# Reordering the seven-product passages of a fused linear-attention and feed-forward kernel

## The chip, the cores and the metric

The kernel runs on one core of a Trainium2 chip. The metric is the device time of one execution in microseconds (us); before the change it is 678.05 us, the median of three runs (677.73 to 678.31). The core has five engines with their own instruction queues: TensorE (PE in the profile, its weight loads PEld), VectorE (DVE), ScalarE (ACT), GpSimd (POOL, here only an issuer of DMAs) and SyncE (SP, also an issuer of DMAs). TensorE writes to PSUM[...].

## What is computed

The reference is a linear attention with decay, whose output is the input of a feed-forward block:

```python
for b in range(nb):                       # blocks of 64 positions, per batch and head
    intra = (qb @ kb.T * Dmask) @ vb
    inter = (qb * lam_pow) @ kv_state
    out[block b] = intra + inter
    kv_state = lam_block * kv_state + (kb * rev_pow).T @ vb
x = out.transpose(0, 2, 1, 3).reshape(3072, 512)
h = x @ w_in                              # 3072 x 2048
g = h - tanh(h)
y = g @ w_out                             # 3072 x 512
```

There are 4 batches, 8 heads, 768 positions and heads of 64; all data are fp32.

## The kernel before

**Groups.** The 3072 tokens are worked on in 6 groups g of 128 positions in 4 batches, 512 tokens each. The attention of group g+1 is cut into pieces (`p0`, `p1`: transposes, scores, outputs, state, sums) that are run between the feed-forward products of group g.

**Seven products.** From group 1 on, each of the two feed-forward products is made by a scheme of Strassen's kind: both factors are cut into 2 x 2 quarters, and seven products of sums of quarters, called P1 to P7 here, take the place of eight. `FACT` (L386) names the factors: P1 = A11 B11, P2 = A12 B21, P3 = S4 B22, P4 = A22 T4, P5 = S1 T1, P6 = S2 T2, P7 = S3 T3. The first product (`up`, L406) is made in four units u of 512 hidden columns. The second (`down`, L602) takes each of its seven products over all units at once.

**Inner seven products.** Some of the seven are cut once more. In the first product from group 2 on, P2 and P4 are made so, for all four units together, ahead of the units (`inner`, L487): seven steps in the order 1, 2, 6, 5, 7, 3, 4 (`STEPS`), step by step for P2 and P4 in turn, P2 with PSUM bank `yb`, P4 with bank `ya`. Their results go to the hidden blocks 11 and 21, which unit 0's P1 and P7 then add to. In the second product P3 to P7 are made so (`down_twice`, L649), with few exceptions (`twice`, L522: P3 and P7 in group 1, P3 in group 5 are plain). Steps 1, 6, 7 and 4 write one y bank in turn (`ya` or `yb`), and ScalarE copies each out (L664); steps 2, 5 and 3 use bank `z` or `w`. Before step 3, VectorE subtracts in place (L666).

**Sums.** `sums_twice` (L641) makes on VectorE what an inner product needs: s1 (L644), s2 (L645), and a21 in place (L646). `sums_once` (L597) makes S2 in place of A11 from S1 (in `down` of P2, L634), and S4 in place of A12 (L801). A last operation of `up` (L454) makes S1 of a unit.

**Weights of the second product.** They come from DRAM in pieces of 256 KB, through a ring of 7 buffers `wb` (`piece`, L565), in the order of one list, `stream`, that `pieces_of` (L525) writes out. GpSimd issues the load of piece i+7 when piece i has been read. A step of an inner product eats one piece, a quarter of a plain product one.

**Order.** The loop from L770 sets the program order of a group: the units; the sums for P4; P2; attention outputs; P4; attention transposes; P5; scores; P6; outputs and state; P7; tokens for the inner products (`inner_tokens`, L475); P3; the next group's `inner`; its unit 0's P1. The scheduler may put an instruction ahead of another on its engine when the latter has to wait, unless the program demands their order; the order found is fixed when the kernel is built. Tiles with few buffers set further waits: each of the banks `ya`, `yb`, `z`, `w` is one, tag `att` has four, the output tiles `o` four, the sums four. P2 of the second product is read out of bank `w` by L632.

**Factors made on the chip.** In groups 1 and 2, `factors_twice` makes the weights of the inner products from their quarters and writes them to DRAM, at set steps of the units (`turns`, L766).

Of the kernel before, what the change touches and what calls it, by code (L numbers as in the profile page):

```python
# [13 lines left out]
AF = mybir.ActivationFunctionType  # L14
AL = mybir.AluOpType
# [8 lines left out]
def kernel(  # L24
# [459 lines left out]

    STEPS = (1, 2, 6, 5, 7, 3, 4)

    def inner(g):  # L487

        y, w, z, r5 = {}, {}, {}, {}
        for n, tag in zip(INNER, ("yb", "ya")):  # L490
            y[n] = bank("y3", tag, 1)
            w[n], z[n] = (bank(x, "att", 4) for x in ("w3", "z3"))
            r5[n] = otile("r5")
        for x in STEPS:
            for n in INNER:
                out4 = hidden(g, 11 if n == 2 else 21)
                c11, c12, c21, c22 = (out4[:, :, i, ts(j, 128)] for i in range(2) for j in range(2))
                b = toks[g, n][x]
                wb = piece(g, ("in", n), x) if x in (3, 5, 6) else None
                dst = w[n] if x == 2 else z[n] if x in (3, 5) else y[n]  # L500
                for u in range(NU):
                    a = wb.rearrange("p m c -> p (m c)")[:, ts(u, 128)] if wb is not None else a_quarter(
                        n, u, *{1: (0, 0), 2: (0, 1), 7: (1, 0), 4: (1, 1)}[x])
                    nc.tensor.matmul(out=dst[:, ts(u, 128)], lhsT=a, rhs=b, start=x in (1, 2, 5) and u == 0, stop=True,  # L504
                                     skip_group_check=True)
                d = dst.rearrange("q (u c) -> q u c", u=NU)
                if x in (1, 4, 6):
                    nc.scalar.activation({1: c11, 4: c21, 6: c12}[x], d, AF.Copy)  # L508
                elif x == 5:
                    nc.scalar.activation(r5[n], dst, AF.Copy)  # L510
                elif x == 7:
                    nc.vector.tensor_tensor(c22, r5[n].rearrange("q (u c) -> q u c", u=NU), d, op=AL.add)
                else:
                    c = c11 if x == 2 else c12
                    nc.vector.tensor_tensor(c, c, d, op=AL.add)

# [3 lines left out]
    def twice(g, n):  # L522
        return n in TWICE and not (g == NG - 1 and n == 3) and not (g == 1 and n in (7, 3))

    def pieces_of(g):  # L525
        if g >= GI:
            yield from ((g, ("in", n), x) for x in (6, 5, 3) for n in INNER)
        if g == 2:
            yield from ((g, ("quarter", t), x) for t in (3, 4) for x in range(4))
        for n in (1, 2, 4, 5, 6, 7, 3):  # L530
            yield from ((g, n, x) for x in (SUB if twice(g, n) else range(NU)))

    stream = [x for g in range(1, NG) for x in pieces_of(g)]
    sent = {"n": 0}
# [67 lines left out]
    def down(g, n):  # L602

        if n in (1, 2):
            t, first = product_bank(("down", g), n)
        else:
            t, first = bank("plain", "w" if n == 7 else "z", 1).rearrange("q (m c) -> q m c", m=2), True
        a = hidden(g, HIDAT[FACT[n][0]])
        for u in range(NU):
            wb = piece(g, n, u)  # L610
            for m in range(2):
                for kt in range(2):
                    nc.tensor.matmul(out=t[:, m, :], lhsT=a[:, u, kt, ts(m, 128)], rhs=wb[:, kt, :],  # L613
                                     start=first and u == 0 and m == 0 and kt == 0, stop=u == NU - 1 and kt == 1,
                                     skip_group_check=True)
        t = t.rearrange("q m c -> q (m c)")
        if n == 1:
            res[g, 1] = otile("q1")
            nc.scalar.activation(res[g, 1], t, AF.Copy)
        elif n == 7:  # L620
            o = otile("q7")
            nc.vector.tensor_tensor(res[g, 4], res[g, 4], t, op=AL.add)
            store(g, 21, res[g, 4])
            nc.vector.tensor_tensor(o, res[g, 5], t, op=AL.add)
            store(g, 22, o)
        elif n == 3:
            o = otile("q3")
            nc.vector.tensor_tensor(o, res[g, 5], t, op=AL.add)
            store(g, 12, o)
        else:  # L630
            o11 = late["pool"].tile([128, 512], F32, name="o11", tag="o11", bufs=1)
            nc.vector.tensor_tensor(o11, res[g, 1], t, op=AL.add)  # L632
            store(g, 11, o11)
            sums_once(g, 11, "S1", 11)  # L634

    def quarter(g, n):

# [11 lines left out]
    def down_twice(g, n, zw):  # L649
        a11, a12, a21, a22 = quarter(g, n)  # L650
        s1, s2 = low.pop((g, n))
        y = bank("y2", "ya" if n in (4, 6, 3) else "yb", 1)[:, 0:128]
        zw = bank("zw", zw, 1)
        o = res[g, n] = otile(f"q{n}")
        r5 = late["pool"].tile([128, 128], F32, name="r5", tag="r5", bufs=2)
        for x, a, dst, keep in ((1, a11, y, o[:, 0:128]), (2, a12, zw[:, 0:128], None), (6, s2, y, o[:, 128:256]),
                                (5, s1, zw[:, 128:256], r5), (7, a21, y, o[:, 384:512]), (3, a12, zw[:, 128:256], None),
                                (4, a22, y, o[:, 256:384])):
            wb = piece(g, n, x).rearrange("p m c -> p (m c)")
            for u in range(NU):  # L660
                nc.tensor.matmul(out=dst, lhsT=a[:, u, :], rhs=wb[:, ts(u, 128)], start=x in (1, 2) and u == 0,  # L661
                                 stop=u == NU - 1, skip_group_check=True)
            if keep is not None:
                nc.scalar.activation(keep, dst, AF.Copy)  # L664
            if x == 2:
                nc.vector.tensor_tensor(a12, a12, s2, op=AL.subtract)  # L666
        nc.vector.tensor_tensor(o[:, 384:512], o[:, 384:512], r5, op=AL.add)
        nc.vector.tensor_tensor(o[:, 0:256], o[:, 0:256], zw[:, 0:256], op=AL.add)
        if n == 6:

            nc.vector.tensor_tensor(o, o, res[g, 1], op=AL.add)
            for x in (4, 5):
                nc.vector.tensor_tensor(res[g, x], res[g, x], o, op=AL.add)
        elif n == 7:
            nc.vector.tensor_tensor(res[g, 4], res[g, 4], o, op=AL.add)
            store(g, 21, res[g, 4])
            nc.vector.tensor_tensor(o, o, res[g, 5], op=AL.add)
            store(g, 22, o)
        elif n == 3:
            nc.vector.tensor_tensor(o, o, res[g, 5], op=AL.add)  # L680
            store(g, 12, o)

    def down_end(g):

# [78 lines left out]
    late["pool"] = ctx.enter_context(tc.tile_pool(name="late", bufs=1))  # L763


    turns, made = {1: (0, (7, 14, 21)), 2: (7 * NU, (2, 7))}, []  # L766
    load_quarters(0)
    load_quarters(1)
    up(1, 0, 1)
    for g in range(1, NG):  # L770
        last = g == NG - 1
        p0, p1 = attention(g + 1) if not last else ([], [])
        for u in range(NU):
            for n in (2, 6, 5, 7, 1, 4, 3) if g < GI else (6, 5, 1, 7, 3) if u + 1 < NU else (6, 5, 7, 1, 3):
                if n != 1:
                    up(g, u, n)
                elif u + 1 < NU:
                    up(g, u + 1, 1)
                else:
                    down(g, 1)  # L780
                if g in turns:
                    made.append(n)
                    step = len(made) - turns[g][0]
                    if step in turns[g][1]:
                        t = turns[g][1].index(step) + len(turns[1][1]) * (g - 1)
                        if t > 2:
                            load_quarters(t)
                        factors_twice(t)
                        if t == 0:
                            load_quarters(2)  # L790
# [2 lines left out]
            if not last and u > 1:  # L793
                run(p0[u - 2:u - 1])
        sums_twice(g, 4)
        down(g, 2)
        run(p0[2:])
        sums_twice(g, 5)
        down_twice(g, 4, "z")
        run(p1[0:1])  # L800
        sums_once(g, 21, 21, 11)  # L801
        sums_twice(g, 6)
        down_twice(g, 5, "w")
        run(p1[1:2])
        if twice(g, 7):
            sums_twice(g, 7)
        down_twice(g, 6, "z")
        if twice(g, 3):
            sums_twice(g, 3)
        run(p1[2:])  # L810
        if twice(g, 7):
            down_twice(g, 7, "w")
        else:
            down(g, 7)
        if not last:
            if g + 1 >= GI:
                inner_tokens(g + 1)
            else:
                up(g + 1, 0, 1)
            if twice(g, 3):  # L820
                down_twice(g, 3, "z")
            else:
                down(g, 3)
            if g + 1 >= GI:
                inner(g + 1)
                up(g + 1, 0, 1)
        else:
            down_end(g)


# [28 lines left out]
```

## Time and profile before

| | |
|---|---|
| Time, median of 3 | 678.05 us |
| Profiled span | 678.3 us |
| TensorE busy | 662.7 us |
| Weight loads busy | 575.2 us |
| VectorE busy | 482.0 us |
| ScalarE busy | 201.3 us |
| DMA, mean over the span | 191 GB/s |
| `wb<-fine`, 154 loads of 256 KB, issue to landing | 4.1 us |

The page is one profiled execution. Busy time is time in which the engine had an instruction of the program in hand; matmuls overlap, so the distance from start to start tells more than their durations. "A<-B" is what an instruction writes and reads. In a timeline the columns are start, time, engine, line, operation, tiles, shape and count; in brackets stands how long the engine was idle before, and what ended the wait. A matmul of the program appears as two records. A step of an inner product is thus 8 records of 128 columns.

### The profile page before, as it was taken

The numbers are of one execution on the slowest core, as the hardware profiler recorded it, in microseconds if no ns is written. First come the engines' busy times: TensorE is split into PE (matmuls) and PEld (weight loads), VectorE is DVE, ScalarE is ACT, GpSimd is POOL, SyncE is SP. The second block draws the span as 40 slices with busy tenths as digits, with TensorE's granted clock in tenths as the row PEclk, the third lists the DMA queues.
The fourth block names the chain that finished last, engine by engine and source line by source line (L and its number), as shares of the span: only waits on it lengthen the run. The fifth ranks groups of instructions, "written<-read, shape, count | busy, mean of one in ns | idle before, by whom it ended". The sixth has DMA issues, their size and how long they took to land.

```text
span 678.3 us, 12940 instructions
## 1 busy us (share of the span) xinstructions
PE 662.7 (98%) x4832; PEld 575.2 (85%) x4832; DVE 482.0 (71%) x878; ACT 201.3 (30%) x398; POOL 201.5 (30%) x348
## 2 busy tenths in 40 slices
PE   6899999999999999999999999999999999999997
PEld 5788855558888899988999988899988899988897
DVE  3797858894889962588986378887358977357753
ACT  2664432423331211343112343112333122334120
POOL 0001424216444434421345200255300244500261
PEclk9999999999999999999999999999999999999999
DMA  9869979958957978686698641698821676700494
GB/s 187 227 195 236 287 215 257 301 142 248 263 173 215 259 208 202 160 238 136 180 277 266 192 82 43 153 284 244 246 42 36 153 240 206 249 22 1 112 303 159
DMA packets 162957, 129.59 MB, mean 191 GB/s; under 512 B 133904, under 2 KB 135056, under 8 KB 162896
## 3 DMA queue, kind: packets, MB, share of 16 engines
q0 software_dynamic: 29216, 97.28, 45.6%
q1 hardware_dynamic: 133536, 31.50, 23.4%
q8 instruction: 38, 0.62, 0.4%
q14 instruction: 23, 0.19, 0.1%
q10 hardware_dynamic: 144, 0.00, 0.0%
HBM read 104.34 MB, written 24.38 MB: 190 GB/s over the span
## 4 chain that ended last, share of the span: by engine, by line
PE 69%; issue 15%; POOL 6%; DMA 6%; DVE 3%; ACT 1%; SPq 0%; POOLq 0%; DVEq 0%; ACTq 0%
PE y L415 13%; PE op L719 8%; PE z L415 8%; PE y L661 7%; PE h L703 6%; PE zw L661 5%; POOL wb L578 5%; PE y L504 3%; PE w L613 3%; PE y L613 3%; PE sp L313 3%; DMA wb<-fine 2%; PE plain L613 2%; DMA raw<-in_moe_w_in_dram 2%; PE op L364 2%
## 5 line engine op out<-in xcount | busy, mean ns | idle before, releaser
L578 POOL DMA_DIRECT2D wb<-fine x154 | 82.9, 538 | 122.0 <-PE y L661 46.3
L423 ACT ACTIVATE th<-g 128x512 f32<-128x512 f32 x76 | 47.3, 630 | 104.5 <-DVE g L428 35.6
L581 POOL DMA_DIRECT2D wb<-factors x52 | 28.2, 543 | 162.0 <-PE y L613 118.1
L415 PE MATMUL y<-xt,w 128*128 128x256 f32 x320 | 73.5, 380 | 0.0
L415 PEld LDWEIGHTS y<-xt,w 128*128 128x128 f32 x320 | 60.5, 190 | 9.4 <-ACT g L508 0.9
L424 DVE TENSOR_TENSOR g<-g,th 128x512 f32<-128x512 f32 x76 | 52.0, 689 | 22.5 <-ACT th L423 22.2
L664 ACT ACTIVATE q<-y 128x128 f32<-128x128 f32 x88 | 24.4, 277 | 115.8 <-PE y L661 114.0
L703 PE MATMUL h<-xt,w 128*128 128x256 f32 x256 | 56.2, 381 | 1.1 <-DVE w L270 1.1
L719 PE MATMUL op<-wt,g 128*128 128x512 f32 x128 | 56.5, 596 | 0.0
L703 PEld LDWEIGHTS h<-xt,w 128*128 128x128 f32 x256 | 48.3, 190 | 8.5 <-DVE w L270 1.5
L661 PE MATMUL y<-wb,g 128*128 128x128 f32 x408 | 54.4, 278 | 1.0 <-DMA wb<-fine 1.0
L661 PEld LDWEIGHTS y<-wb,g 128*128 128x128 f32 x408 | 49.3, 192 | 2.4 <-issue 1.5
L719 PEld LDWEIGHTS op<-wt,g 128*128 128x128 f32 x128 | 23.8, 190 | 27.7 <-issue 26.5
L415 PE MATMUL z<-tt,ws 128*128 128x256 f32 x160 | 38.7, 380 | 0.0
L317 DVE TENSOR_TENSOR ss<-sp,mask 128x512 f32<-128x512 f32 x48 | 30.8, 681 | 10.6 <-PE sp L313 10.6
L415 PE MATMUL y<-tt,ws 128*128 128x256 f32 x160 | 38.2, 382 | 0.0
L415 PE MATMUL z<-xt,ws 128*128 128x256 f32 x160 | 37.9, 380 | 0.0
L661 PE MATMUL zw<-wb,g 128*128 128x128 f32 x272 | 36.1, 276 | 0.6 <-DMA wb<-fine 0.5
L197 POOL DMA_DIRECT2D raw<-in_moe_w_out_dram x16 | 8.8, 553 | 92.7 <-ACT r L261 59.9
L613 PE MATMUL w<-wb,g 128*128 128x256 f32 x160 | 35.8, 382 | 0.0
L613 PE MATMUL y<-wb,g 128*128 128x256 f32 x160 | 35.4, 379 | 0.0
L415 PEld LDWEIGHTS y<-tt,ws 128*128 128x128 f32 x160 | 30.1, 190 | 5.4 <-DVE g L428 1.5
(169 smaller groups left out, 1290.5 us busy)
## 6 DMA issues: line engine op xcount, KB each, us to landing
wb<-fine POOLq DMA_DIRECT2D x154, 256.0 KB, 4.1
wb<-factors POOLq DMA_DIRECT2D x60, 256.0 KB, 4.4
raw<-in_moe_w_out_dram POOLq DMA_DIRECT2D x16, 512.0 KB, 5.1
v_nat<-in_v_dram SPq DMA_DIRECT2D x24, 256.0 KB, 5.3
factors<-wt POOLq DMA_DIRECT2D x8, 768.0 KB, 5.5
wb<-fine_in POOLq DMA_DIRECT2D x24, 256.0 KB, 5.4
k_nat<-in_k_dram SPq DMA_DIRECT2D x20, 256.0 KB, 5.4
raw<-in_moe_w_in_dram SPq DMA_DIRECT2D x8, 512.0 KB, 5.8
```

Source lines behind the costliest of these rows:

```text
L313: nc.tensor.matmul(out=sp[j][:, p, :], lhsT=kt[ts(j, 64), p, :], rhs=qt[ts(j, 64), p, :], start=True, stop=True)
L317: nc.vector.tensor_tensor(ss[:, j], sp[j], mask[:, j], op=AL.mult)
L415: nc.tensor.matmul(out=t[:, m, :], lhsT=wt[:, kt, ts(m, 128)], rhs=x[:, kt, :], start=first and m == 0 and kt == 0, stop=kt == 1, skip_gro ...
L423: nc.scalar.activation(th, src, AF.Tanh)
L424: nc.vector.tensor_tensor(dst(c), src, th, op=AL.subtract)
L578: nc.gpsimd.dma_start(out=t.rearrange("p m c -> p (m c)"), in_=fine[TWICE.index(n_), SUB.index(x_)].rearrange("p u c -> p (u c)"))
L581: nc.gpsimd.dma_start(out=t, in_=factors[XAT[FACT[n_][1]]][:, 2 * x_:2 * x_ + 2, :])
L613: nc.tensor.matmul(out=t[:, m, :], lhsT=a[:, u, kt, ts(m, 128)], rhs=wb[:, kt, :], start=first and u == 0 and m == 0 and kt == 0, stop=u = ...
L661: nc.tensor.matmul(out=dst, lhsT=a[:, u, :], rhs=wb[:, ts(u, 128)], start=x in (1, 2) and u == 0, stop=u == NU - 1, skip_group_check=True)
L664: nc.scalar.activation(keep, dst, AF.Copy)
L703: nc.tensor.matmul(out=hm[:, m, :], lhsT=w1[u][:, i, a, ts(m, 128)], rhs=xt[0, t][:, i, :], start=m == 0 and i == 0, stop=i == KI - 1, ski ...
L719: nc.tensor.matmul(out=obank[b], lhsT=g, rhs=wt[:, 2 * a:2 * a + 2, :], start=kt == 0 and a == 0, stop=kt == KH - 1 and a == 1)
```

## The change

It puts four things in another order and leaves every matmul as it is.

- P2 of the second product is made between P4 and P5, no longer ahead of P4. The sums for S2 (`sums_once(g, 11, "S1", 11)`) leave `down` and are called behind P4. The list of weight pieces follows.
- The inner P2 and P4 of the next group's first product are no longer made in turn with each other. `inner` becomes a generator for one of them, `inner_steps`. P2 is made step by step in turn with P3 of the second product, which also becomes a generator.
- P4 follows, in turn with P1, P6 and P5 of unit 0, which leave the first round of the unit loop. Both inner products use bank `yb`.
- The steps at which group 2 makes its factors move by one (`turns`).

It is meant to spread the demand for weight pieces over more of TensorE's time, and to put other work between operations that share a bank.

```diff
-    def inner(g):
-        y, w, z, r5 = {}, {}, {}, {}
-        for n, tag in zip(INNER, ("yb", "ya")):
...
+    def inner_steps(g, n, tag):
+        y, w, z, r5 = bank("y3", tag, 1), bank("w3", "att", 4), bank("z3", "att", 4), otile("r5")
...
+            yield
...
+    def in_turn(g):
+        if twice(g, 3):
+            return [a for x in STEPS for a in (("down", x), ("in", x))]
+        return [("down", 0), ("in", 1), ("in", 2), ("down", 1), ("in", 6), ("in", 5), ("down", 2), ("in", 7), ("in", 3),
+                ("down", 3), ("in", 4)]
...
     def pieces_of(g):
         if g >= GI:
-            yield from ((g, ("in", n), x) for x in (6, 5, 3) for n in INNER)
+            yield from ((g, ("in", 4), x) for x in (6, 5, 3))
...
-        for n in (1, 2, 4, 5, 6, 7, 3):
+        for n in (1, 4, 2, 5, 6, 7):
             yield from ((g, n, x) for x in (SUB if twice(g, n) else range(NU)))
...
-    turns, made = {1: (0, (7, 14, 21)), 2: (7 * NU, (2, 7))}, []
+    turns, made = {1: (0, (7, 14, 21)), 2: (7 * NU, (1, 6))}, []
...
-            for n in (2, 6, 5, 7, 1, 4, 3) if g < GI else (6, 5, 1, 7, 3) if u + 1 < NU else (6, 5, 7, 1, 3):
+            for n in (2, 6, 5, 7, 1, 4, 3) if g < GI else (1, 7, 3) if u == 0 else (6, 5, 1, 7, 3) if u + 1 < NU else (
+                    6, 5, 7, 1, 3):
...
         sums_twice(g, 4)
-        down(g, 2)
+        every(down_twice(g, 4, "z"))
         run(p0[2:])
+        sums_once(g, 11, "S1", 11)
         sums_twice(g, 5)
-        down_twice(g, 4, "z")
+        every(down(g, 2))
         run(p1[0:1])
...
+        p3 = down_twice(g, 3, "z") if twice(g, 3) else down(g, 3)
+        p2 = inner_steps(g + 1, 2, "yb")
+        for kind, _ in in_turn(g):
+            next(p3 if kind == "down" else p2)
+        every(p2)
+        every(p3)
+        p4 = inner_steps(g + 1, 4, "yb")
+        for n in (None, None, 1, None, None, 6, None, None, 5, None):
+            if n is None:
+                next(p4)
             else:
-                up(g + 1, 0, 1)
...
+                up(g + 1, 0, n)
+        every(p4)
```

More of the change, by code (lines that the diff above doesn't have):

```diff
@@ L485 @@
     STEPS = (1, 2, 6, 5, 7, 3, 4)
-    def inner(g):
-        y, w, z, r5 = {}, {}, {}, {}
-        for n, tag in zip(INNER, ("yb", "ya")):
-            y[n] = bank("y3", tag, 1)
-            w[n], z[n] = (bank(x, "att", 4) for x in ("w3", "z3"))
-            r5[n] = otile("r5")
-        for x in STEPS:
[L495 to L515, printed above, removed]
@@ new lines, in inner_steps @@
+    def inner_steps(g, n, tag):
+        y, w, z, r5 = bank("y3", tag, 1), bank("w3", "att", 4), bank("z3", "att", 4), otile("r5")
+        out4 = hidden(g, 11 if n == 2 else 21)
+        c11, c12, c21, c22 = (out4[:, :, i, ts(j, 128)] for i in range(2) for j in range(2))
+        for x in STEPS:
+            b = toks[g, n][x]
+            wb = piece(g, ("in", n), x) if x in (3, 5, 6) else None
+            dst = w if x == 2 else z if x in (3, 5) else y
+            for u in range(NU):
+                a = wb.rearrange("p m c -> p (m c)")[:, ts(u, 128)] if wb is not None else a_quarter(
+                    n, u, *{1: (0, 0), 2: (0, 1), 7: (1, 0), 4: (1, 1)}[x])
+                nc.tensor.matmul(out=dst[:, ts(u, 128)], lhsT=a, rhs=b, start=x in (1, 2, 5) and u == 0, stop=True,
+                                 skip_group_check=True)
+            d = dst.rearrange("q (u c) -> q u c", u=NU)
+            if x in (1, 4, 6):
+                nc.scalar.activation({1: c11, 4: c21, 6: c12}[x], d, AF.Copy)
+            elif x == 5:
+                nc.scalar.activation(r5, dst, AF.Copy)
+            elif x == 7:
+                nc.vector.tensor_tensor(c22, r5.rearrange("q (u c) -> q u c", u=NU), d, op=AL.add)
+            else:
+                c = c11 if x == 2 else c12
+                nc.vector.tensor_tensor(c, c, d, op=AL.add)
+            yield
@@ L523, in twice @@
         return n in TWICE and not (g == NG - 1 and n == 3) and not (g == 1 and n in (7, 3))
+    def in_turn(g):
[3 more added lines that the diff above has]
+                ("down", 3), ("in", 4)]
     def pieces_of(g):
         if g >= GI:
-            yield from ((g, ("in", n), x) for x in (6, 5, 3) for n in INNER)
+            yield from ((g, ("in", 4), x) for x in (6, 5, 3))
         if g == 2:
             yield from ((g, ("quarter", t), x) for t in (3, 4) for x in range(4))
-        for n in (1, 2, 4, 5, 6, 7, 3):
+        for n in (1, 4, 2, 5, 6, 7):
             yield from ((g, n, x) for x in (SUB if twice(g, n) else range(NU)))
+        if g == NG - 1:
+            yield from ((g, 3, x) for x in range(NU))
+            return
+        for kind, x in in_turn(g):
+            if kind == "down":
+                yield g, 3, x
+            elif x in (3, 5, 6):
+                yield g + 1, ("in", 2), x
     stream = [x for g in range(1, NG) for x in pieces_of(g)]
@@ L615, in down @@
                                      skip_group_check=True)
+            if u + 1 < NU:
+                yield
         t = t.rearrange("q m c -> q (m c)")
@@ L633, in down @@
             store(g, 11, o11)
-            sums_once(g, 11, "S1", 11)
+        yield
     def quarter(g, n):
@@ L666, in down_twice @@
                 nc.vector.tensor_tensor(a12, a12, s2, op=AL.subtract)
+            if x != STEPS[-1]:
+                yield
         nc.vector.tensor_tensor(o[:, 384:512], o[:, 384:512], r5, op=AL.add)
@@ L681, in down_twice, with every @@
             store(g, 12, o)
+        yield
+    def every(steps):
+        for _ in steps:
+            pass
     def down_end(g):
@@ L779 @@
                 else:
-                    down(g, 1)
+                    every(down(g, 1))
                 if g in turns:
@@ L802 @@
         sums_twice(g, 6)
-        down_twice(g, 5, "w")
+        every(down_twice(g, 5, "w"))
         run(p1[1:2])
@@ L806 @@
             sums_twice(g, 7)
-        down_twice(g, 6, "z")
+        every(down_twice(g, 6, "z"))
         if twice(g, 3):
@@ L810 @@
         run(p1[2:])
[L811 to L817, printed above, removed]
-            else:
-                up(g + 1, 0, 1)
[L820 to L828, printed above, removed]
+        every(down_twice(g, 7, "w") if twice(g, 7) else down(g, 7))
+        if last:
+            down_end(g)
+            continue
+        inner_tokens(g + 1)
+        p3 = down_twice(g, 3, "z") if twice(g, 3) else down(g, 3)
[8 more added lines that the diff above has]
+                next(p4)
+            else:
+                up(g + 1, 0, n)
+        every(p4)
 _INS = ['q', 'k', 'v', 'lam', 'moe_w_in', 'moe_w_out']
```

## The prediction

> **What bounds the kernel now.** I read the page first, its busy line and its chain.
>
> ```profile
> PE 662.7 (98%) x4832; PEld 575.2 (85%) x4832; DVE 482.0 (71%) x878; ACT 201.3 (30%) x398; POOL 201.5 (30%) x348
> ...
> PE 69%; issue 15%; POOL 6%; DMA 6%; DVE 3%; ACT 1%; SPq 0%; POOLq 0%; DVEq 0%; ACTq 0%
> ```
>
> TensorE is the bound, and the diff leaves its matmuls as they are: every product keeps its count and shape. So the change can only remove or add holes in TensorE's stream. I looked for the holes in the PE timeline from 155 us on (group 1 to the end). A matmul record of 128 columns starts 0.112 us after the one before, one of 256 columns 0.216 us (medians of start to start), so a step of an inner product (8 records) takes 0.89 us and a 512-row product 6.9 us; what exceeds that is a hole, together with the some 0.1 us that the next record is late. The page's own waits name only the largest:
>
> ```profile
> PE zw L661 <- issue: 1.4, 1, 1.4
> ...
> PE y L661 <- DMA wb<-fine: 1.0, 1, 1.0
> PE zw L661 <- DMA wb<-fine: 0.5, 1, 0.5
> ```
>
> Summed with the smaller ones, in us: group 1, in P4 and P5 of the second product, 0.33 (228.0), 0.41 (232.8), 1.62 (235.1), and 0.35 at the state product (249.9); group 2, 0.30 (299), 0.49 over P5 (340 to 343), 0.37 in P3 (367); group 3, 0.17 in P5 (446) and 1.22 in P3 (475.5); group 4, 0.23; group 5, 0.76 in P7 (665); and 0.24 in each of four passages to the next group, where unit 0's P6 waits for VectorE to read P1's bank. That is 7.2 us: 670.8 is the floor of any gain.
>
> Two of them, as the timelines have them. Group 3's P3, last step, late because its weight piece had not landed:
>
> ```profile
> 474.76 1.06 PE L661 MATMUL zw<-wb,g 128*128 128x128 f32 x8
> 476.80 1.13 PE L661 MATMUL y<-wb,g 128*128 128x128 f32 x8 [0.98 <-DMA wb<-fine]
> ```
>
> And the largest, which is not a weight at all. P5's step 3 in group 1 reads what L666 makes, and L666 stands on VectorE behind a transpose that waits for a block of k:
>
> ```profile
> 234.75 0.71 DVE L293 STREAM_TRANSPOSE kt<-k_blk 128x512 f32<-128x512 f32 x1 [1.41 <-DMA k_nat<-in_k_dram]
> 235.39 0.65 DVE L303 TENSOR_TENSOR qd<-qt,fwd 128x512 f32<-128x512 f32 x1
> 235.96 0.68 DVE L666 TENSOR_TENSOR gS<-gS,s 128x512 f32<-128x512 f32 x1
> ```
>
> TensorE starts that step at 236.74, just after.
>
> [...] the start-to-start times above leave only 7.2 us of holes, so I go by those. [...] L666 above sat behind a stalled transpose. [...] the rows here have 676 to 693, and back to back they follow every 0.60 us. [...] The second inner product of the passage is made on one y bank instead of two, with other work between its steps.
>
> **The change part by part.**
>
> *P3 in turn with the next group's P2.* Removed: P3's seven steps alone, each eating one 256 KB piece in 0.89 us, with six more pieces behind them. Now P3's 7 pieces and P2's 3 are spread over 14 steps of 0.89 us. The pieces land a median 4.1 us after issue, up to 5.9 in group 3, and the ring of 7 gives 7 x 0.89 = 6.2 us of notice where every step eats a piece; with 10 pieces in 14 steps it gives 8.7 us. Group 3's 1.22 and group 2's 0.37 go: **-1.6**. Each y bank has three other steps (2.7 us) between its uses, as before for P2, and its evacuation takes 0.60 us on ScalarE: free. P2 writes hidden block 11, whose last reader, P6, is long past: free. Its VectorE adds fall where VectorE has little (6.4 us busy in 371 to 391): free. Its spare tile r5 waits for the store of quarter 21 to land (366.70 to 371.50 in group 2); its copy comes 7.1 us after P7's end, at about 372, so a wait of up to 0.5 us on ScalarE, with P3's copies behind it, whose bank is needed only 3 steps on: nothing.
>
> *P4 in turn with unit 0.* Between P1 and P6 now stand two steps of P4 (1.8 us), in which VectorE reads P1's bank (L428, 0.69): four times 0.24, **-0.95**. P4's first step shares bank yb with P2's last, whose copy takes 0.60 us; in the trace unit 0's P5 already slips in ahead of P1 in the same situation (277.86), so I cost it at nothing; the other end is 0.7 four times.
>
> *P2 of the second product between P4 and P5.* Its four slow pieces (1.73 us each) now let the ring fill ahead of P5, P6, P7: P5's holes in groups 2 and 3 go, **-0.65**. In group 5 the hole of P7 (0.76) comes at the end of 21 fast steps instead of 28: I take it, **-0.75**, other end 0.
>
> What it adds is that P4 starts right behind the scores, where VectorE makes P4's sums. Group 2 before:
>
> ```profile
> 318.25 0.69 DVE L645 TENSOR_TENSOR s<-s,g 128x512 f32<-128x512 f32 x1
> ...
> 320.13 0.69 DVE L451 TENSOR_TENSOR g<-g,z 128x512 f32<-128x512 f32 x1 [0.60 <-PE z L415]
> 321.58 0.69 DVE L424 TENSOR_TENSOR g<-g,th 128x512 f32<-128x512 f32 x1 [0.76 <-ACT th L423]
> 322.19 0.68 DVE L317 TENSOR_TENSOR ss<-sp,mask 128x512 f32<-128x512 f32 x1
> 322.79 0.68 DVE L454 TENSOR_TENSOR gS<-g,g 128x512 f32<-128x512 f32 x1
> ...
> 324.59 1.28 DVE L317 TENSOR_TENSOR ss<-sp,mask 128x512 f32<-128x512 f32 x2
> 325.79 0.68 DVE L646 TENSOR_TENSOR g<-g 128x512 f32<-128x512 f32 x1
> ```
>
> P4 would start at 322.0, where P2 did. Step 6 (323.8) finds s2 made at 318.9. Step 7 (due 325.6) needs L646, which overwrites what L454 must read first and comes after four score products: done at 326.5, so 0.9 us late in groups 2, 3 and 4. The attention products (L358, 1.03 us) are ready then and can stand in for it; I take a third of 2.7: **+0.9**, ends 0 and 2.7. P5's step 2 now waits for L632 to read bank w, P2's: 0.89 us of step 1 against 0.69 plus whatever stands before it on VectorE: **+0.2** in all, ends 0 and 0.6 each in four groups.
>
> Group 1 is worse off:
>
> ```profile
> 212.15 0.69 DVE L424 TENSOR_TENSOR g<-g,th 128x512 f32<-128x512 f32 x1 [0.76 <-ACT th L423]
> ...
> 217.97 0.68 DVE L644 TENSOR_TENSOR s<-g 128x512 f32<-128x512 f32 x1
> 218.57 0.68 DVE L600 TENSOR_TENSOR g<-gS,g 128x512 f32<-128x512 f32 x1
> 219.17 0.68 DVE L645 TENSOR_TENSOR s<-s,g 128x512 f32<-128x512 f32 x1
> ```
>
> There P4 would start at 212.6 and want s2 at 214.4, and s2 is done at 219.9: 5.5 us, of which the attention products (L358 and L364, 3 us) can fill the larger part. But P5's step 3 was bound by the block of k at 234.75 anyhow, so a delay of some 2 us before it runs into the 2.4 us of holes that stood there. I take **0**; ends -1.6 (the sums are made earlier) and +3.6 (L632 gets behind that transpose: P5's step 2 at about 236.7 instead of 231.1, with the four steps that had filled the wait, 3.6 us, still to come).
>
> Sum: -1.6 - 0.95 - 0.65 - 0.75 + 0.9 + 0.2 = -2.85: 678.05 - 2.85 = **675.2**.
>
> **The rivals.** *Fuller gain:* group 1's holes close as well (-1.6), and none of the +1.1 comes: 678.05 - 3.95 - 1.6 = 672.5. For it: the order on TensorE bends around waits already. Against: k lands when SyncE's queue brings it. *Even:* the ring's holes go, but P4's sums cost their full 2.7 and group 5's hole stays: -2.85 + 1.8 + 0.75 = -0.3, 677.75. For it: the 0.9 us is read straight from rows. *VectorE becomes the bound behind P4 (the other side):* group 1 +3.6, L646 +2.7, L632 4 x 0.6 = 2.4, against -3.95: +4.75, 682.8. For it: VectorE has no gap from 321.6 to 333.6[...], and in group 1 the k transposes can be placed ahead of L632, since they are ready to go while P2 still runs. Against: after that stretch VectorE has 12 us of work in the 18 us to P2's new end, so it should be free for L632.
>
> **How the numbers follow.** Forecast 0.46, fuller gain 0.10, even 0.14, slower 0.30. The slower case reaches from +1.5 (group 1 alone, partly) to +8, so half of it lies under 681.8; the range goes from 671.8, just under the fuller gain, to 681.8. Faster 0.56, same (within 1.36 us) 0.14, slower 0.30.
>
> **What would show it.** Right: no wait of P3 for a weight piece in groups 2 and 3; the passage without the wait for L428; P5 without holes in groups 2 and 3. Wrong: a hole at P4's step 6 in group 1 longer than 2.5 us, holes at P4's step 7 near 0.9 in groups 2 to 4, P5's step 2 waiting for L632, L632 behind L293 in group 1. If TensorE's busy time without holes changes by over 1 us, switching between shapes costs something that I set at nothing.

## The result: slower, and where the profile after puts the time

The changed kernel takes **687.27 us** (median of four runs, 686.68 to 688.76), the kernel before 677.89 in four runs beside it (677.07 to 678.31): a ratio of 1.0143 [1.0123, 1.0163]. The forecast was 675.2, the range ended at 681.8; it is the side of the third rival, by more than that rival gave.

The page of the kernel after, its busy line and its chain:

```profile
PE 667.6 (97%) x4832; PEld 578.7 (85%) x4832; DVE 481.1 (70%) x878; ACT 200.9 (29%) x398; POOL 201.5 (29%) x348
...
PE 85%; issue 8%; DMA 3%; POOL 2%; DVE 1%; ACT 1%; SPq 0%; POOLq 0%; ACTq 0%
```

TensorE has the same 4832 records, but they keep it busy 4.9 us longer than before: a part of the loss isn't idle time at all. The rest shows in TensorE's waits (columns: microseconds in all, number of waits, longest):

```profile
PE y L674 <- ACT r L677: 2.1, 3, 0.7
PE zw L674 <- DVE s L657: 1.9, 1, 1.9
PE w L624 <- DMA wb<-factors: 0.8, 1, 0.8
PE y L415 <- ACT g L443: 0.7, 1, 0.7
```

None of the four was there before; the wait of 1.4 us in P5 of group 1 is gone, and the waits of L661 for `wb<-fine` (1.5 us) are down to 0.4. In the new file the inner product's matmul is L674 (before: L661), the sums s1, s2 and a21 are L657, L658 and L659 (L644 to L646), the subtraction ahead of step 3 is L679 (L666), the reader of P2's bank L645 (L632), and the plain product L624 (L613).

To see where the time went, I cut the span at the first matmul of P1 and of P7 of the second product in each group, and added the stretches. The column e0 is a second profile of the kernel before; it shows what of the first is chance. In e1 only P2 was moved; in e2 only the passage between the groups was put in turn. A bank is here a PSUM tile of 128 x 512 fp32.

| us, from the traces | before | e0 | after | e1 | e2 |
|---|---|---|---|---|---|
| start to P1 of group 1 | 200.2 | 200.5 | 199.6 | 200.8 | 200.5 |
| P1 to P7, group 1 | 51.29 | 50.47 | 54.64 | 53.08 | 51.31 |
| P1 to P7, groups 2, 3, 4 together | 138.83 | 138.50 | 142.71 | 142.71 | 139.53 |
| P7 to the next P1, four passages | 236.44 | 235.67 | 234.94 | 237.29 | 234.92 |
| P1 of group 5 to the end | 48.51 | 48.64 | 49.93 | 49.99 | 48.53 |
| end of the last matmul | 675.2 | 673.8 | 681.8 | 683.9 | 674.8 |

After minus before is 3.35 in group 1, 3.88 in groups 2 to 4 and 1.42 in group 5; 1.50 is won in the passages, and the first row differs by chance, since nothing was changed there. The loss lies in the stretches where P2 was moved. The last matmul ends 6.5 us later than in the first profile of before and 8.0 later than in e0, while the medians differ by 9.4: the profiled run of before, at 680.09 us, was slower than its other runs.

**Groups 2 to 4: a step behind VectorE.** TensorE's timeline of group 2 in the kernel after, and VectorE's beside it:

```profile
328.22 1.06 PE L674 MATMUL zw<-wb,s 128*128 128x128 f32 x8
330.00 1.13 PE L674 MATMUL y<-wb,g 128*128 128x128 f32 x8 [0.72 <-ACT r L677]
330.96 1.06 PE L674 MATMUL zw<-wb,g 128*128 128x128 f32 x8
```

```profile
326.22 0.68 DVE L454 TENSOR_TENSOR gS<-g,g 128x512 f32<-128x512 f32 x1
326.82 0.68 DVE L317 TENSOR_TENSOR ss<-sp,mask 128x512 f32<-128x512 f32 x1
327.42 0.68 DVE L455 TENSOR_TENSOR g<-g,g 128x512 f32<-128x512 f32 x1
328.02 1.28 DVE L317 TENSOR_TENSOR ss<-sp,mask 128x512 f32<-128x512 f32 x2
329.21 0.68 DVE L659 TENSOR_TENSOR g<-g 128x512 f32<-128x512 f32 x1
```

Step 7 of P4 would follow 0.89 us after 328.22, at 329.11; it starts at 330.00, just after L659 ends at 329.89. L659 is ready when L454 has read what it overwrites, but the scheduler has placed four score products and L455 ahead of it. The trace names ScalarE's copies L677 as the releaser, but the one that frees bank y ended at 328.70 and the last one at 329.60; L659 ends last, and e4 below shows that the hole goes when L659 comes earlier. The same hole of 0.88 us stands at 435.4 and 541.8, in groups 3 and 4, and the step after it follows in 0.96 instead of 0.89.

**P5 and the scores: a product cut in two.** Before, P5's last steps ran through and the scores followed as one block of 32 records. After (group 2, TensorE, then VectorE):

```profile
347.44 1.06 PE L674 MATMUL y<-wb,gS 128*128 128x128 f32 x8
348.43 0.49 PE L313 MATMUL sp<-qt,kt 64*128 64x128 f32 x4
348.86 0.94 PE L674 MATMUL y<-wb,gS 128*128 128x128 f32 x6
349.63 1.06 PE L674 MATMUL zw<-wb,gS 128*128 128x128 f32 x8
350.53 0.39 PE L674 MATMUL y<-wb,gS 128*128 128x128 f32 x2
350.85 1.83 PE L313 MATMUL sp<-qt,kt 64*128 64x128 f32 x28
```

```profile
343.92 0.69 DVE L645 TENSOR_TENSOR o<-q,w 128x512 f32<-128x512 f32 x1 [1.04 <-PE w L624]
344.52 0.71 DVE L293 STREAM_TRANSPOSE qt<-q_blk 128x512 f32<-128x512 f32 x1
...
348.70 0.68 DVE L679 TENSOR_TENSOR gS<-gS,s 128x512 f32<-128x512 f32 x1
```

VectorE begins the attention transposes only behind L645, which waits for the last matmul of P2 until 343.92; six operations of theirs then stand ahead of L679, and step 3 (349.63) is put off behind it. TensorE doesn't idle: four score records and six of the eight of step 4 are moved ahead. But the scores now stand in two pieces, and each piece brings late starts of some 0.1 to 0.2 us (348.86, for one, is 0.43 us after 348.43, where four score records take 0.25).

In group 4 the account closes. P1 to P7 takes 44.81 us there in before, e0 and e2, and 46.33 in the changed kernel and in e1. The 1.52 us are 0.95 for the hole at step 7 with the late step behind it, 0.41 for the cut scores (measured in e5 below), and 0.16 for P5's second step, which waits until L645 has read bank w.

**Group 1: the hole, and a slower clock after it.** TensorE, VectorE, and one row of the table of windows (columns: window, its length, busy time and instructions of PE, PEld, DVE, ACT, POOL, then the granted clock, the DMA share and GB/s):

```profile
215.13 1.09 PE L364 MATMUL op<-ss,v_nat 128*64 128x128 f32 x16
218.12 1.99 PE L674 MATMUL zw<-wb,s 128*128 128x128 f32 x8 [1.89 <-DVE s L657]
220.04 0.69 PE L364 MATMUL op<-ss,v_nat 128*64 128x128 f32 x2
220.66 1.62 PE L674 MATMUL y<-wb,s 128*128 128x128 f32 x8
```

```profile
217.38 0.68 DVE L657 TENSOR_TENSOR s<-g 128x512 f32<-128x512 f32 x1
217.98 0.68 DVE L337 TENSOR_TENSOR state<-state,fwd 128x512 f32<-128x512 f32 x1
218.59 0.68 DVE L658 TENSOR_TENSOR s<-s,g 128x512 f32<-128x512 f32 x1
```

```profile
218.00:222.00 4.00, 3.88 (x17) 3.33 (x18) 3.90 (x8) 0.28 (x1) 1.08 (x2) 0.57 0.49 124
```

P4's two steps that read sums are reordered (step 5, which reads s1, ahead of step 6, which reads s2), the attention products L358 and half of L364 are drawn ahead, and still TensorE stands for 2.07 us until s1 ends at 218.06. Behind it P4 and the rest of L364 alternate in small pieces. From 218.24 on the trace has half clock for 3.41 us: the eight records at 218.12 take until 220.04, where those of e1, after the same hole, take 1.09 us. P5 itself starts at 234.54 (before: 230.24), and VectorE's wait for the block of k is gone, since the transposes come later (in the second row no idle time stands):

```profile
234.74 0.69 DVE L645 TENSOR_TENSOR o<-q,w 128x512 f32<-128x512 f32 x1 [1.03 <-PE w L624]
...
237.76 0.67 DVE L293 STREAM_TRANSPOSE kt<-k_blk 128x512 f32<-128x512 f32 x1
```

**Group 5: a step drawn ahead of its weights.** Without attention to fill with, the scheduler put the first four records of P2 into the middle of P4, and their piece hadn't landed:

```profile
643.30 1.06 PE L674 MATMUL zw<-wb,s 128*128 128x128 f32 x8
645.13 1.13 PE L624 MATMUL w<-wb,g 128*128 128x256 f32 x4 [0.77 <-DMA wb<-factors]
646.10 1.05 PE L674 MATMUL y<-wb,g 128*128 128x128 f32 x8
```

That is a hole of 0.94 us, and another of 0.56 before P7's first step (661.2) takes the place of the 0.76 at its step 3.

**The passage works as meant.** Group 3's P3, where 1.22 us were lost before, alternates with P2 at 0.89 us a step:

```profile
482.74 1.06 PE L674 MATMUL y<-wb,g 128*128 128x128 f32 x8
483.63 0.61 PE L499 MATMUL y<-xt,w 128*128 128x128 f32 x4
```

From P7 to the next P1 it takes 58.13 us into groups 3 to 5; before, 58.25 to 59.71. Only the passage into group 2 has grown (60.54 against 59.86), by a new wait of 0.85 us at 301.6 that the experiments explain.

### The profile page after: what moved, and what is told of

It is laid out like the page before. It is cut to its first block, busy times and chain, and to the rows that moved or that the text cites. A ratio compares the mean times of both kernels' runs of the same rounds, so it can differ in the third digit from the quotient of the medians.

```text
span 684.9 us, 12915 instructions
## 1 busy us (share of the span) xinstructions
PE 667.6 (97%) x4832; PEld 578.7 (85%) x4832; DVE 481.1 (70%) x878; ACT 200.9 (29%) x398; POOL 201.5 (29%) x348
## 4 chain that ended last, share of the span: by engine, by line
PE 85%; issue 8%; DMA 3%; POOL 2%; DVE 1%; ACT 1%; SPq 0%; POOLq 0%; ACTq 0%
PE y L415 13%; PE y L674 11%; PE h L723 8%; PE z L415 8%; PE op L739 8%; PE zw L674 8%; PE w L624 4%; PE y L624 4%; PE y L499 4%; PE sp L313 3%; PE op L364 3%; PE plain L624 2%; PE z L499 2%; PE op L358 1%; PE kv L333 1%
## 5 line engine op out<-in xcount | busy, mean ns | idle before, releaser
L415 PE MATMUL y<-xt,w 128*128 128x256 f32 x320 | 74.0, 381 | 0.7 <-ACT g L443 0.7
L677 ACT ACTIVATE q<-y 128x128 f32<-128x128 f32 x88 | 24.4, 277 | 157.9 <-PE y L674 157.1
L415 PEld LDWEIGHTS y<-xt,w 128*128 128x128 f32 x320 | 59.8, 190 | 10.0 <-ACT g L443 1.1
L674 PE MATMUL y<-wb,g 128*128 128x128 f32 x408 | 54.7, 279 | 2.5 <-ACT r L677 2.1
L674 PEld LDWEIGHTS y<-wb,g 128*128 128x128 f32 x408 | 49.4, 192 | 4.7 <-ACT r L677 2.6
L415 PE MATMUL z<-tt,ws 128*128 128x256 f32 x160 | 38.1, 381 | 0.0
L415 PE MATMUL z<-xt,ws 128*128 128x256 f32 x160 | 38.0, 380 | 0.0
L415 PE MATMUL y<-tt,ws 128*128 128x256 f32 x160 | 38.0, 379 | 0.0
L624 PE MATMUL w<-wb,g 128*128 128x256 f32 x160 | 36.3, 383 | 0.8 <-DMA wb<-factors 0.8
L674 PE MATMUL zw<-wb,g 128*128 128x128 f32 x272 | 36.3, 276 | 0.0
L624 PE MATMUL y<-wb,g 128*128 128x256 f32 x160 | 35.4, 379 | 0.0
L624 PEld LDWEIGHTS w<-wb,g 128*128 128x128 f32 x160 | 29.8, 190 | 5.3 <-DMA wb<-factors 1.0
```

The costliest lines, as they stand in the source:

```text
L415: nc.tensor.matmul(out=t[:, m, :], lhsT=wt[:, kt, ts(m, 128)], rhs=x[:, kt, :], start=first and m == 0 and kt == 0, stop=kt == 1, skip_gro ...
```

## The experiments

The theory after the result: the passage is about neutral, and the move of P2 costs everything, in three parts: P4's sums on VectorE (groups 1 to 4), L679 behind the transposes (all groups with attention), and changes of tile shape, which no row calls a wait. The rivals: the passage has shifted the ring of weights against the groups, and P2 would be harmless without it; or the loss is chance of the profiled run. Times of the kernel before in these sessions: 679.3 (22 and 37 runs).

**e0: the kernel before, profiled again.** No edit.

> The kernel before, unchanged, profiled a second time. Its first profiled run took 680.09 us where its other runs took 677.1 to 678.3, and the span of the changed kernel's profile is only 6.6 us longer where the times differ by 9.4. Theory A (the first profile of before held some 2 us of chance holes): the span is near 676 and the holes at DMA-fed steps (1.62 in group 1, 1.22 in group 3, 0.76 in group 5) are smaller by 2 us or more in all. Theory B (the holes are the program's own): span 678, the same holes at the same steps.

678.64 us, span 676.9. Counted with the late record behind them, as in the prediction: group 3's hole of 1.22 is not there (below); group 2's in P3 is 0.83 instead of 0.37; that of group 1, where VectorE waits 0.53 us for the block of k and not 1.41, is 1.28 instead of 1.62; in group 5 two of 0.34 and 0.53 stand instead of 0.76:

```profile
474.39 1.06 PE L661 MATMUL zw<-wb,g 128*128 128x128 f32 x8
475.29 1.06 PE L661 MATMUL y<-wb,g 128*128 128x128 f32 x8
```

So waits for DMA, of weight pieces above all, come and go from run to run, and the prediction took those of one trace for holes of every run. The holes of VectorE's making (0.14 before L415 at unit 0's P6, 0.20 before z at 298) are in both.

**e1 and e2: each half of the change alone.**

```diff
 e1, against the kernel before
-        for n in (1, 2, 4, 5, 6, 7, 3):
+        for n in (1, 4, 2, 5, 6, 7, 3):
...
-        down(g, 2)
+        down_twice(g, 4, "z")
         run(p0[2:])
+        sums_once(g, 11, "S1", 11)
         sums_twice(g, 5)
-        down_twice(g, 4, "z")
+        down(g, 2)
 e2, against the kernel after
-        for n in (1, 4, 2, 5, 6, 7):
+        for n in (1, 2, 4, 5, 6, 7):
...
-        every(down_twice(g, 4, "z"))
+        every(down(g, 2))
...
-        every(down(g, 2))
+        every(down_twice(g, 4, "z"))
```

> The kernel before with one part of the change alone: P2 of the second product between P4 and P5 (with its list of pieces and the place of the S2 sums); the passage to the next group as before. Theory A (the move is the whole loss: P4 behind the scores waits for VectorE's sums, and TensorE's order is broken into small pieces): by the two traces the stretches from the end of P1 to P7 lost 3.4, 1.0, 1.3, 1.5 and 1.4 us in groups 1 to 5, 8.6 in all, so 686 to 687. Theory B (the passage in turn loses, by bank yb alone and by changes of shape): within 2 us of 678.

> The changed kernel with P2 put back ahead of P4; the passage in turn stays. Theory A: 676 to 678, since the passage was 0.1 to 1.6 us shorter in three groups and 0.7 longer in one by the traces; no hole at P4's steps. Theory B: 684 or more.

e1 took 688.55 us, 1.0114 [1.0072, 1.0155]; e2 678.82, 0.9994 [0.9977, 1.001]; both lie a little above what was expected. The move of P2 is the whole loss, and P1 to P7 of groups 2 to 4 is the same 142.71 us in e1 and in the kernel after: the passage has no part in it. e1 even ends later than the kernel after, because the old passage still waits for pieces (1.51 us in group 2's P3, at 373.9). e2 is worth nothing measurable as a whole. It has the wait of the passage into group 2 too:

```profile
297.96 1.46 PE L415 MATMUL y<-tt,ws 128*128 128x256 f32 x6
300.10 1.13 PE L415 MATMUL y<-xt,w 128*128 128x256 f32 x4 [0.69 <-ACT g L443]
```

**e4: the sums for P4 ahead of the last scores.**

```diff
+            if u == NU - 1:
+                sums_twice(g, 4)
...
             if not last and u > 1:
                 run(p0[u - 2:u - 1])
-        sums_twice(g, 4)
```

(The call stands ahead of `inner_weights(u)` too.)

> The changed kernel with P4's sums (s1, s2 and the in-place a21) called ahead of the last scores and of the last inner weights of group 1, so that they come earlier in VectorE's queue; nothing else. Theory A, in the form that VectorE's place for these sums makes the holes: the 2.1 us hole at P4's step 6 in group 1 and the 0.9 at step 7 in groups 2, 3 and 4 go or shrink to 0.3, together some 4 us: 683 to 684. If the cost is instead in the changes between shapes on TensorE, under 1.5 us is won: 686 or more.

684.04 us, 1.0063 [1.0043, 1.0084]; 3.2 us less than the change in full. Group 1's hole before step 5 is gone, and there is no half clock (1.00 from 200 to 226 us); 0.50 us before step 7 and 1.54 before step 3 stand in its place. In groups 2 to 4 the hole of 0.88 at step 7 gives way to one of 0.59 at step 3:

```profile
327.82 1.06 PE L674 MATMUL y<-wb,g 128*128 128x128 f32 x8
329.30 1.13 PE L674 MATMUL zw<-wb,g 128*128 128x128 f32 x8 [0.42 <-ACT q L677]
```

L659 is made in time now, and L679 behind it isn't: two score products stand between them. In neither of the two orders that were tried is VectorE's stretch behind the scores short enough for P4; the wait moves one operation on.

**e5: the transposes ahead of P2.**

```diff
+        run(p1[0:1])
         every(down(g, 2))
-        run(p1[0:1])
```

> The changed kernel with the attention's transposes of the second half called ahead of P2 instead of behind it; nothing else. In the changed kernel VectorE makes six transposes and decays (3.7 us) right behind P2, ahead of the subtraction that P5's step 3 needs, and TensorE's order was built around that: two score products, then a part of step 4, stand ahead of step 3. Theory A (that break costs the 0.6 us by which P5 and the scores together are longer than 8.3 us): the stretch from P1 to P7 gets 0.6 us shorter in groups 1 to 4, 2.4 us in all, so 684 to 686. Rival (the break is free and the loss is only in P4's waits): no change, 687.

685.15 us, 1.0072 [1.0047, 1.0097]; P5 and the scores run through again (the last two steps of P5 and the scores of group 2):

```profile
348.93 1.06 PE L674 MATMUL y<-wb,gS 128*128 128x128 f32 x8
349.92 2.06 PE L313 MATMUL sp<-qt,kt 64*128 64x128 f32 x32
```

P1 to P7 is shorter by 0.41 us in each of groups 2 to 4 (48.19 to 47.78 in groups 2 and 3, 46.33 to 45.92 in group 4), and by 0.42 in group 1, 1.65 in all where 2.4 were expected. That is the price of one more cut between shapes, without any idle wait.

**e6: both edits, and P2 moved only in groups 2 to 4.**

```diff
-        for n in (1, 4, 2, 5, 6, 7):
+        for n in (1, 2, 4, 5, 6, 7) if g in (1, NG - 1) else (1, 4, 2, 5, 6, 7):
```

(and the calls of groups 1 and 5 in the order of before, the others as in e4 and e5.)

> The changed kernel with all that seemed to cost mended: P4's sums ahead of the last scores, the transposes ahead of P2, and P2 moved in groups 2 to 4 only (in groups 1 and 5 it stays ahead of P4). Theory A (the loss was those waits and breaks, not the place of P2 as such): about the time with P2 not moved at all, plus 0.6 us of wait at P4's step 3 in three groups less some 0.5 of weight waits in P5: 678 to 680. Rival (the place of P2 costs by itself, as by weights that come late): 682 or more.

680.86 us, 1.0024 [1.0008, 1.0039], just above what was expected; the runs with a mean granted clock above 0.997 have medians of 679.91 us and, for the kernel before, 679.14. Most of the loss is gone, as the parts said; what remains are three holes of 0.59 and one of 0.85 in the passage into group 2, and the passages' gain doesn't pay for them. So even the mended move is no gain.

**e7: shape changes by themselves.** The kernel before, with the second half of the scores cut into six pieces between P6's steps: the same matmuls, five more changes there and back in each of groups 1 to 4.

```diff
+            if n == 6 and pending:
+                for _ in range({1: 1, 2: 1, 6: 1, 5: 1, 7: 2}.get(x, 0)):
+                    next(pending[0])
...
```

(`pending` holds the scores, made a generator that stops after each piece.)

> The kernel before with the second half's score products of groups 1 to 4 cut into 6 pieces, which stand between the steps of P6 instead of in one block ahead of it: 5 more changes from 128-row to 64-row products and back in each group, 20 in all, with all inputs ready and no work added. Theory A (TensorE loses time at each such change, about 0.2 us for there and back, as read off the changed kernel): 4 us longer, 681 to 683, and the stretch from P1 to P7 longer by 1.0 us in each group. Rival (changes are free, what was lost in the changed kernel are hidden waits): 678 and the same stretch within 0.3.

686.95 us, 1.0103 [1.0071, 1.0136], twice what I expected. Its TensorE timeline, and e0's at the same place:

```profile
349.01 0.49 PE L315 MATMUL sp<-qt,kt 64*128 64x128 f32 x4
349.43 1.16 PE L680 MATMUL zw<-wb,g 128*128 128x128 f32 x8
350.52 0.49 PE L315 MATMUL sp<-qt,kt 64*128 64x128 f32 x4
350.94 1.16 PE L680 MATMUL y<-wb,s 128*128 128x128 f32 x8
```

```profile
345.34 2.06 PE L313 MATMUL sp<-qt,kt 64*128 64x128 f32 x32
347.32 1.16 PE L661 MATMUL y<-wb,g 128*128 128x128 f32 x8
```

A period of one step and four score records is 1.51 us (349.43 to 350.94). The step alone takes 0.89; four score records, at the 0.06 us that the block of 32 shows (1.98 / 32), 0.25: the change there and back costs some **0.4 us**, half of it on each side (score records 1.09 us after a step's start instead of 0.89; a step 0.42 us after them instead of 0.25). P1 to P7 is longer than in e0 by 2.22, 2.35, 2.16 and 1.97 us in groups 1 to 4, 0.39 to 0.47 for each of the five, chance waits of either trace included. No wait is shown for the changes; they appear as busy time. Between products of 128 and 256 columns, both on 128 rows, the passage of the changed kernel shows nothing of the kind: the steps of P4 and the products of unit 0 alternate there at 0.89 and 1.73 us, what they take alone:

```profile
386.24 1.06 PE L499 MATMUL z<-tt,wb 128*128 128x128 f32 x8
387.14 1.89 PE L415 MATMUL y<-tt,ws 128*128 128x256 f32 x8
388.87 1.05 PE L499 MATMUL y<-tt,w 128*128 128x128 f32 x8
```

**e9: e2 with group 2's factors at the old step numbers.** The count runs over the products of the unit loop, and P6 and P5 of unit 0 have left it: step 1 now stands behind P1 of unit 1, step 2 behind P7 of unit 0; before, step 2 stood behind P5 of unit 0.

```diff
-    turns, made = {1: (0, (7, 14, 21)), 2: (7 * NU, (1, 6))}, []
+    turns, made = {1: (0, (7, 14, 21)), 2: (7 * NU, (2, 7))}, []
```

> The passage in turn alone (P2 not moved), with group 2's factors made at steps 2 and 7 of its count as in the kernel before, not at 1 and 6. In the passage into group 2, the trace of the passage alone has a 0.85 us hole in unit 0, where P7 waits for ScalarE to read P6's bank. If the early factors on VectorE delay that, the hole goes: the stretch from P7 of group 1 to P1 of group 2 is 59.7 instead of 60.5, and the time 0.7 us shorter. If not, no change.

**676.85 us, 0.996 [0.9942, 0.9977]**: faster than both kernels, if only by 0.4% against the kernel before. The wait at 300.1 is gone, and the passage into group 2 takes 59.44 us, not 60.53:

```profile
298.24 1.89 PE L415 MATMUL z<-tt,ws 128*128 128x256 f32 x8
299.97 2.32 PE L415 MATMUL y<-xt,w 128*128 128x256 f32 x10
```

In e2 the four subtractions that make the factors (L572) stand on VectorE ahead of L451, which empties bank z. P5 needs that bank and can't follow P6. The scheduler put half of the next product on bank y there instead, and that one has to wait until ScalarE has copied P6 out of the bank (L443, from 299.45 to 300.05, right after P6's end). In e9 L451 comes before P5 is due, and P5 covers the copy. L451 in e2 and in e9:

```profile
300.17 0.68 DVE L451 TENSOR_TENSOR g<-g,z 128x512 f32<-128x512 f32 x1
```

```profile
296.82 0.68 DVE L451 TENSOR_TENSOR g<-g,z 128x512 f32<-128x512 f32 x1
```

So the passage in turn is worth some 2.5 us (2.3 among the runs with a mean granted clock above 0.997), and the place of the factors had eaten most of it.

## Why the prediction was wrong

Against the trace that it was made from, the changed kernel's last matmul ends 6.5 us later, where 2.85 us less were forecast.

- **P4's sums in groups 2 to 4: +0.9 taken, +2.9 measured.** The step was read right (L646 behind four score products, 0.9 us late, three times) and then cut to a third, because attention products were ready to stand in. None did: the order is fixed when the kernel is built, and there the scheduler drew nothing ahead, as it did in group 1. Each hole is 0.88, and 0.07 for the late step behind it.
- **Group 1: 0 taken, +3.35 measured.** The hole was foreseen at 5.5 - 3 = 2.5 us and measured 2.07. What failed is "a delay of some 2 us before it runs into the 2.4 us of holes that stood there". Those holes did go, but the delay at P5's start was 4.9 us (P5's start less P1's: 30.1 before, 35.0 after): the hole, 1.6 us of half clock in the profiled run (group 1 of e1, without it, is 1.56 shorter), and a rest of 1.3. For that, P4 cut up by attention products is the likely cause: from P1 to P5 e1 has 13 changes between tile shapes where the kernel before has 5, and 1.3 us for eight more is 0.16 each, near the 0.2 of e7.
- **Changes of shape: costed at nothing.** One in each of groups 1 to 4 at P5, 1.6 us by e5, and those in group 1's P4. The last sentence of the prediction had named busy time as the sign; it rose by 4.9 us, of which the half clock and longer records behind waits are a part.
- **Group 5: -0.75 taken, +1.42 measured.** I looked at P7's hole alone, and not at where the scheduler could draw P2's steps: P4 has a wait, P2 is at hand, and the order is decided without knowing when a piece lands.
- **The ring's -1.6 and -0.65.** Both mechanisms are in the traces: P3 runs without a wait in every group, and so does P5 in groups 2 to 4 of the changed kernel, where e2 has 0.48 and 0.39. The single holes were chance: e0 has neither the 1.22 in P3 nor a wait for a piece in P5 of groups 2 and 3. The size of the first term was right all the same. The two passages into groups 3 and 4 take 116.27 us together in all six traces with the passage in turn, and 117.57 to 119.17 in the four without it.
- **The passage, -0.95 taken.** The waits for L428 are gone, but the passage of 58.25 us that held only such a wait became 58.13: 0.12 each, not 0.24. That the factors in their new place would hold up VectorE's reading of bank z, and with it the passage into group 2 (0.85 us), was not seen at all; the diff's `turns` line was read and not costed.
- **P5's step 2 and bank w, +0.2 taken.** In groups 1 to 4 step 2 starts 0.95 us after step 1, and step 6, the third, 0.99 after that: 0.16 each, 0.6 in all. The wait was read right, the late records behind it weren't counted. L632 did not get behind a stalled transpose; that part of the third rival didn't occur.

The third rival had the right side and the right engine, VectorE behind P4. Its +3.6 for group 1 and +2.7 for L646 came nearly to size, the first for other reasons; its 2.4 for L632 didn't. That the time lies above its 682.8 is the gains' doing: it subtracted 3.95, of which the traces show 1.5 in the passages, some 0.7 in P5 of groups 2 and 3, and in group 5 a loss; and it had no term for the changes of shape.

Half clock follows group 1's hole in the profiled runs of the changed kernel and of e5, and not in that of e1 (last section). The changed kernel's four runs have mean clocks of 0.998, 1.0, 0.998 and 0.995, and the one without a drop (686.68 us) is only 0.09 us below the next, so the loss doesn't hang on it; in e5 the one run at 1.0 took 683.34 us, the six at 0.997 and 0.998 684.91 to 685.72. What stays open: that the 1.3 us of group 1 come from its changes of shape was argued from e1's rows, not shown by a run of its own.

## What to carry to other kernels

Before moving a product ahead, look at what the engine that makes its operands is doing at that moment: here P2, which needed one subtraction only, had been the cover for VectorE's sums, and the other order behind the scores that was tried only moved the wait on. On a TensorE that is 98% busy, count the changes of tile shape of the new order beside its waits, for they are shown as busy time (here some 0.4 us there and back). And take waits for DMA as a gain only at the size that they have over several profiles of the same kernel, since single ones come and go; where a diff of several parts mixes gain and loss, run the parts, for the best version here was a half of the change with one of its lines taken back.

## What the runs showed of the hardware

**Changes of shape.** A change between score products on 64 rows and products on 128 rows cost 0.4 us there and back, seen in five places of each group of e7 (0.39 to 0.47 each) and once more in e5's difference (0.41); a change between 128 and 256 columns alone cost nothing in the changed kernel's passage (0.89 and 1.73 us, as alone).

**The clock.** In the profiled run of the changed kernel, TensorE stood for 2.07 us and then had half clock from 218.24 us on, for 3.41 us. In that of e5 the clock fell a little later; in that of e1, with the same hole, it did not fall. TensorE's idle time and the mean granted clock, from the tables of windows:

| trace | idle in 214 to 218, us | idle in 218 to 222, us | clock in 218 to 222 | clock in 222 to 226 |
|---|---|---|---|---|
| after | 1.77 | 0.12 | 0.57 | 1.00 |
| e5 | 1.65 | 0.23 | 0.74 | 0.84 |
| e1 | 0.50 | 1.39 | 1.00 | 1.00 |
| e4 | 0.34 | 1.38 | 1.00 | 1.00 |

The idle time of the three traces with the hole is the same to 0.01 us (1.88 to 1.89 in all), and group 1 of e1 is 1.56 us shorter than that of the changed kernel. Why the clock fell in two of them and not in the third was not shown. The kernel before has runs with a lower clock too: a mean of 0.997 or less in 14 of its 59 runs, with a median of 681.3 us against 679.14 for the others. At which place it fell in them no trace shows.
